# Attention and two MLP layers on one core: layer two's second products in seven partial products of 256 columns

## The chip, the cores and the metric

One core of a Trainium2 chip runs the whole program in one launch. The time is device time in microseconds (us); the kernel before took 741.88 us, the median of 3 runs (741.71 to 742.18).

## The reference

```python
def reference(**kw):                       # cut to the shapes and the arithmetic
    # attention: 2 batches x 8 heads x 768 positions x 64; a query sees the keys of its own cluster
    attn_out = _attn_ref(q, k, v, centroids)
    x = attn_out.transpose(0, 2, 1, 3).reshape(1536, 512)
    h = x @ moe_w_in                       # 1536x512 @ 512x2048, layer one
    x = np.maximum(0.01 * h, h) @ moe_w_out        # @ 2048x512
    h = x @ moe2_w_in                      # layer two, the same shapes
    r = np.maximum(h, 0.0)
    return (r * r) @ moe2_w_out
```

All of it is float32. The kernel splits each operand of a product into a high part (fp32r) and a low part and adds three products, high x high, high x low and low x high.

## The kernel before, in words

After the attention come two layers, `m` = 0 and 1. The 2048 hidden columns are 16 blocks `f` of 128, taken in pairs (`f`, `f` + 1); the 1536 rows are three parts `b` of 512. For each pair and each `b` the first product gives a hidden tile of 128 x 512 in one of four PSUM banks U, V, W, X (tag `h0` to `h3`); the activation splits it into `gh` and `gl`; the second product goes from these into four banks `o0` to `o3`, and a flush adds them to the sums `acc` in SBUF.

Three forms of a pair exist. A plain pair computes everything directly. A quad pair (`quad`, layer two from `f` = 2 on) computes the first product of `b` = 0 and 1 with seven products in place of eight (the Strassen-Winograd form of a 2 x 2 block product: P1 to P7, with differences of the inputs `th`, `tl` and of the weights, block `(m, f, 2)`), and its second products directly: `g2` issues for each hidden tile four slices of three matmuls, 512 columns wide. A pair of `seven` (layer one, `f` = 4 to 14) does the same for the second products too: differences T1 to T4 of the hidden tiles B11, B12, B21, B22, seven products M1 to M7 with a fourth weight block `(m, f, 3)`, and after each product the bank's contents, a partial sum, are added to `acc` (r1 to r7, two each). `b` = 2 is always direct: u0, u1 are its hidden tiles, o0 to o3 its second products, f0 to f3 their flushes. In the plain and quad forms the second products of `b` = 2 are done in the next pair (`behind`).

In `seven` the order of all engines is written out in one string of names: SEVEN_FIRST, then SEVEN_REST. Every engine takes its own instructions in that order. A name ending in `h` writes `gh` on ScalarE, in `f` the full value on ScalarE, in `l` the low part `gl` (GpSimd for B11, T1, T2, T3, VectorE otherwise); k and a are copies and sums of partial products on ScalarE and VectorE; T1 to T4 and the r and f flushes are on VectorE. n0.0 to n3.4 prepare the weight blocks of the next pair (c: this pair, l: the one after): for blocks 0 and 1 the steps are .0 the load, .1 "mag" on ScalarE and "low" on GpSimd (of the raw words in `wraw`), .2 the join of both on VectorE, .3 the high part on ScalarE, .4 the low part on GpSimd; for blocks 2 and 3 (differences) .0 is four sums on GpSimd, .1 the high part, .2 the low part. The two layers' activations read:

```python
        def prelu(out, x):                                   # in seven, before
            nc.scalar.activation(out=out, in_=x, func=AF.Prelu, alpha=0.01)
        def square():                                        # in acts, layer two
            nc.vector.scalar_tensor_tensor(
                out=h, in0=h, scalar=0.0, in1=t, op0=ALU.max, op1=ALU.mult)
```

In layer two the activation of `acts` is a relu on ScalarE into a buffer `t`, the square on VectorE, the high part on ScalarE, the low part on VectorE. In layer one the stationary operand of the second product is the weight slice and the moving one is the hidden tile (out: columns x rows); in layer two it is a slice of 128 rows of `gh` or `gl`, and the moving one is the weight (out: rows x columns), so that the result can be stored as it is.

Of the kernel before, what the change touches and what calls it, by code (L numbers as in the profile page):

```python
# [80 lines left out]
) + SEVEN_REST + " h4.0 h4.1"  # L81
DOTS = {(0, 0): 0, (0, 1): 1, (1, 0): 2}
# [3 lines left out]
def attention_moe_moe_kernel(  # L86
# [26 lines left out]
    SEVEN = (4, 6, 8, 10, 12, 14)  # L113
# [44 lines left out]
    for m in range(2):  # L158
        for f in range(0, NF, 2):
            blocks += [(m, f, 0), (m, f, 1)]  # L160
            if f >= PLAIN[m] * 2:
                blocks.append((m, f, 2))
            if m == 0 and f in SEVEN:
                blocks.append((m, f, 3))
# [842 lines left out]
    def last_rows(b):  # L1007

        banks = [(ps_o, "o0"), (ps_o, "o1"), (ps_o, "o2"), (ps_l, "o3")]
        pair = [(parts.pop((1, b, f)), weights[1, NF - 2, f % 2]) for f in (NF - 2, NF - 1)]  # L1010
        for o in range(4):
            ts = slice(o * 128, (o + 1) * 128)
            for i in range(2 if o == 3 else 1):
                c = slice(i * N // 2, (i + 1) * N // 2) if o == 3 else slice(0, N)
                if i:
                    ps = bank(0)
                else:
                    pool, tag = banks[o]
                    ps = pool.tile([128, N], F32, tag=tag, name="o")
                ps = ps[:, 0 : c.stop - c.start]  # L1020
                n = 0
                for (gh, gl), (wh, wl) in pair:
                    w = slice(DM + c.start, DM + c.stop)
                    for l, r in (
                        (gh[:, ts], wh[:, w]), (gh[:, ts], wl[:, w]), (gl[:, ts], wh[:, w])
                    ):
                        nc.tensor.matmul(out=ps, lhsT=l, rhs=r, start=(n == 0), stop=(n == 5))  # L1027
                        n += 1
                flush(1, b, NF // 2 - 1, o, ps, c)

# [30 lines left out]
    def quad(m, f):  # L1061
        f0, f1, s = ((m, f, j) for j in range(3))
        k2 = range(2)

        def p(out, w, x, first):
            product(out, [w(k) for k in k2], [x(k) for k in k2], first)

        def add(out, a, b):
            nc.vector.tensor_tensor(out=out, in0=a, in1=b, op=ALU.add)

        U, V, W, X = (bank(i) for i in range(4))

        def first():
            p(U, lambda k: w_in(f0, k), lambda k: x_in(k, 0), True)
            p1 = tmp()
            nc.scalar.copy(out=p1, in_=U)
            p(V, lambda k: w_in(f0, 2 + k), lambda k: x_in(2 + k, 0), True)
            add(V, V, p1)
            act(m, 0, f, V)

        kept = []

        def second():
            for q, i, o, fresh in ((U, 2, 1, False), (W, 0, 0, True)):
                p(q, lambda k: w_in(s, i + k), lambda k: t_in(o, k), fresh)
                kept.append(tmp())
                nc.scalar.copy(out=kept[-1], in_=q)

        def third():
            u2, p5 = kept  # L1090
            p(U, lambda k: w_in(s, 4 + k), lambda k: t_in(2, k), False)
            add(X, U, p5)
            x = acts(m, 1, f + 1, X)
            w = acts(m, 1, f, W)
            u = acts(m, 0, f + 1, U)
            if m:
                x.pop(0)()
            p(W, lambda k: w_in(s, 6 + k), lambda k: x_in(2 + k, 1), False)
            if m:
                x.pop(0)()  # L1100
            x.pop(0)()
            add(W, W, u2)
            if m:
                w.pop(0)()
            p(U, lambda k: w_in(f1, 2 + k), lambda k: t_in(3, k), False)
            if m:
                u.pop(0)()
            x.pop(0)()
            for q in (w, u):
                if m:  # L1110
                    q.pop(0)()
                q.pop(0)()
            w.pop(0)()
            u.pop(0)()

        return first, second, third

    def seven(f, prev, after, later):

        f0, f1, si, so = ((0, f, j) for j in range(4))  # L1120
# [45 lines left out]
        def prelu(out, x):  # L1166
            nc.scalar.activation(out=out, in_=x, func=AF.Prelu, alpha=0.01)
# [3 lines left out]
        def high(n, x, active=False):  # L1171
            hi[n] = gg.tile([128, N], F32R, tag="gh", name="gh")
            lo[n] = gg.tile([128, N], F32R, tag="gl", name="gl")
            if active:
                prelu(hi[n], x)
            else:
                nc.scalar.copy(out=hi[n], in_=x)
# [4 lines left out]
        def active(n, x, sbuf=False):  # L1182
            full[n] = tmp("t", 3) if sbuf else x
            prelu(full[n], x)
# [32 lines left out]
        def second(out, ws, g, fresh, stop=True):  # L1217
            wh, wl = ws
            mm = ((wh, hi[g]), (wh, lo[g]), (wl, hi[g]))
            for i, (l, r) in enumerate(mm):  # L1220
                nc.tensor.matmul(  # L1221
                    out=out, lhsT=l, rhs=r, start=(fresh and i == 0), stop=(stop and i == 2),
                    skip_group_check=True,
                )

        def w_out(block, c):
            return tuple(w[:, c : c + 128] for w in weights[block])

        def seventh(q, block, c, g, fresh):
            if fresh:  # L1230
                for j in range(2):
                    i = 2 * "AB".index(q) + j
                    st[q, j] = (ps_l if i == 3 else ps_o).tile(
                        [128, N], F32, tag=f"o{i}", name="o"
                    )
            for j in range(2):
                second(st[q, j], w_out(block, c + 128 * j), g, fresh)

        for name, q, block, c, g, b, half in (
# [8 lines left out]
            for j in range(2):  # L1248
                g = f // 2 if f < NF - 2 or name in "2347" else 1
                ops[f"r{name}.{j}"] = lambda q=q, j=j, b=b, g=g, o=2 * half + j: flush(  # L1250
                    0, b, g, o, st[q, j], later=x_low if b == 0 and o > 1 else None
                )

        def last(o):
            ps = st["o", o] = bank((3, 2, 3, 2)[o])
            c = DM + o * 128
            second(ps, w_out(f0, c), "u0", True, False)
            second(ps, w_out(f1, c), "u1", False)

# [85 lines left out]
    def step_list(m, f, prev):  # L1345
# [9 lines left out]
        if f < 2 * PLAIN[m]:  # L1355
            seq = [unit(0, 0), unit(0, 1)]
            if behind:
                seq[1:1] = behind[:1]
                seq += behind[1:]
            seq += [unit(1, 0), out_of(0, 0)]  # L1360
            if m:
                held = []

                def start():
                    held.extend(acts(m, 1, f + 1, g1(m, 1, f + 1)))
                    for g in held[:2]:
                        g()

                def out_and_end():
                    out_of(0, 1)()  # L1370
                    for g in held[2:]:
                        g()

                seq += [start, out_and_end]
            else:
                seq += [unit(1, 1), out_of(0, 1)]
            seq += [unit(2, 0), out_of(1, 0), unit(2, 1), out_of(1, 1)]
            return seq, tail

        first, second, third = quad(m, f)  # L1380
        seq = [
            first, behind[0], second, behind[1], third,
            out_of(0, 0), unit(2, 0), out_of(0, 1), unit(2, 1), out_of(1, 0), out_of(1, 1),
        ]
        if f == NF - 2:
            return seq + [lambda: last_rows(2)], []
# [44 lines left out]
    for m in range(2):  # L1431
        turn = 0
        for f in range(0, NF, 2):
# [13 lines left out]
            if m == 0 and f in SEVEN:  # L1447
                seven(f, prev, after, later)
# [3 lines left out]
            for i, step in enumerate(seq):  # L1452
# [12 lines left out]
                if m == 0 and i == 8 and f + 2 == SEVEN[0]:  # L1465
# [50 lines left out]
```

## Time and profile before

| | |
|---|---|
| median of 3 runs | 741.88 us (741.71 to 742.18) |
| the profiled execution | 742.35 us, of which 740.4 us span |
| TensorE busy | 733.9 us (99%) |
| VectorE, ScalarE, GpSimd busy | 545.7, 454.8, 503.7 us |
| granted TensorE clock | 1.00 of full speed over the span |

The profile follows one execution. An engine is busy while one of its instructions is under way; matmuls overlap in the pipe, so their rate is read from one start to the next, not from their duration. The chain of waits goes back from the last instruction to what released each step. In the lists by time, what stands in brackets at a row's end is the idle time before it and what ended it. Layer one ends 485.46 us after the span's start; layer two's pairs begin at 485.46 (plain), 512.66, 543.94, 575.22, 606.50, 637.78, 669.06 and 700.34.

### The profile page before, as it was taken

The numbers are of one execution on the slowest core, as the hardware profiler recorded it, in microseconds if no ns is written. First come the engines' busy times: TensorE is split into PE (matmuls) and PEld (weight loads), VectorE is DVE, ScalarE is ACT, GpSimd is POOL, SyncE is SP. The second block draws the span as 40 slices with busy tenths as digits, with TensorE's granted clock in tenths as the row PEclk, the third lists the DMA queues.
The fourth block names the chain that finished last, engine by engine and source line by source line (L and its number), as shares of the span: only waits on it lengthen the run. The fifth ranks groups of instructions, "written<-read, shape, count | busy, mean of one in ns | idle before, by whom it ended". The sixth has DMA issues, their size and how long they took to land.

```text
span 740.4 us, 11210 instructions
## 1 busy us (share of the span) xinstructions
PE 733.9 (99%) x4012; PEld 640.5 (87%) x4012; DVE 545.7 (74%) x856; ACT 454.8 (61%) x841; POOL 503.7 (68%) x471
## 2 busy tenths in 40 slices
PE   9999999999999999999999999999999999999998
PEld 8999999999998888888888888888888888888886
DVE  7999999999997535477776866887666666676655
ACT  7988988988998564446365363657634435443330
POOL 6999999999957648776787877899534343343400
PEclk9999999999999999999999999999999999999999
DMA  5694474572603311112121131111312112121004
GB/s 149 166 215 120 108 187 110 110 186 67 172 1 116 113 58 58 57 58 82 62 86 57 58 114 57 58 58 57 112 45 73 58 58 85 44 99 58 1 0 171
DMA packets 16727, 65.52 MB, mean 88 GB/s; under 512 B 3120, under 2 KB 4272, under 8 KB 11680
## 3 DMA queue, kind: packets, MB, share of 16 engines
q1 hardware_dynamic: 16672, 64.81, 29.7%
q8 instruction: 32, 0.52, 0.3%
q14 instruction: 23, 0.19, 0.1%
HBM read 43.02 MB, written 3.15 MB: 62 GB/s over the span
## 4 chain that ended last, share of the span: by engine, by line
PE 94%; POOL 2%; DVE 2%; ACT 1%; issue 1%; DMA 0%; POOLq 0%; ACTq 0%
PE h L919 33%; PE o L997 21%; PE A L583 8%; PE S L486 8%; PE o L1221 8%; PE T L548 7%; PE h L1221 4%; PE S L356 2%; PE warm L296 1%; PE o L1027 1%; ACT e L518 1%; POOL e L535 1%; DVE el L565 1%; DVE nm L508 0%; DMA hb<-spl 0%
## 5 line engine op out<-in xcount | busy, mean ns | idle before, releaser
L173 POOL TENSOR_TENSOR wl<-wt,wh 128x1024 fp32r<-128x1024 f32 x31 | 75.9, 2448 | 59.8 <-ACT wh L172 59.1
L1037 DVE TENSOR_TENSOR acc<-o,acc 128x512 f32<-128x512 f32 x160 | 103.6, 684 | 11.9 <-PE o L997 11.9
L919 PE MATMUL h<-xh,wl 128*128 128x512 f32 x288 | 112.4, 390 | 0.0
L919 PE MATMUL h<-xl,wh 128*128 128x512 f32 x288 | 112.3, 390 | 0.0
L919 PE MATMUL h<-xh,wh 128*128 128x512 f32 x288 | 112.1, 391 | 0.0
L565 DVE TENSOR_TENSOR el<-T,eh 128x512 fp32r<-128x512 f32 x144 | 94.5, 682 | 2.8 <-ACT eh L559 2.1
L535 POOL TENSOR_SCALAR e<-e,r 128x768 f32<-128x768 f32 x96 | 86.2, 908 | 12.7 <-PE T L548 6.8
L508 DVE TENSOR_REDUCE nm<-S 128x1 f32<-128x768 f32 x96 | 90.8, 947 | 3.7 <-PE S L356 1.9
L518 ACT ACTIVATE e<-S,nm 128x768 f32<-128x768 f32 x96 | 87.2, 908 | 10.0 <-DVE ds L384 3.6
L486 PE MATMUL S<-hb 128*128 128x384 f32 (+1 forms) x384 | 89.5, 347 | 0.5 <-DMA hb<-spl 0.4
L559 ACT CAST eh<-T 128x512 fp32r<-128x512 f32 x144 | 79.5, 590 | 8.9 <-PE T L548 8.7
L583 PE MATMUL A<-eh,vv 128*128 128x256 f32 x288 | 80.4, 308 | 0.6 <-DVE xt L605 0.6
L548 PE MATMUL T<-ident,e 128*128 128x128 f32 x576 | 79.7, 274 | 0.6 <-POOL e L535 0.6
L583 PE MATMUL A<-el,vv 128*128 128x256 f32 x288 | 73.0, 283 | 0.2 <-DVE el L565 0.2
L968 DVE TENSOR_TENSOR gl<-h,gh 128x512 fp32r<-128x512 f32 x60 | 40.8, 690 | 43.8 <-ACT h L963 24.5
L548 PEld LDWEIGHTS T<-ident,e 128*128 128x128 f32 x576 | 68.9, 143 | 3.6 <-POOL e L535 0.7
L997 PE MATMUL o<-wh,gl 128*128 128x512 f32 x184 | 71.7, 390 | 0.0
L997 PE MATMUL o<-wh,gh 128*128 128x512 f32 x184 | 71.7, 389 | 0.0
L997 PE MATMUL o<-wl,gh 128*128 128x512 f32 x184 | 71.7, 389 | 0.0
L173 POOL TENSOR_TENSOR wl<-ws,wh 128x1024 fp32r<-128x1024 f32 x18 | 43.3, 2403 | 41.3 <-ACT wh L172 41.3
L953 ACT ACTIVATE t<-h 128x512 f32<-128x512 f32 x48 | 28.1, 600 | 67.5 <-PE h L919 33.9
L919 PEld LDWEIGHTS h<-xh,wh 128*128 128x128 f32 x288 | 54.1, 188 | 11.9 <-DVE gl L1180 0.9
(187 smaller groups left out, 1763.7 us busy)
## 6 DMA issues: line engine op xcount, KB each, us to landing
wraw<-w SPq DMA_DIRECT2D x32, 1024.0 KB, 4.7
hb<-spl SPq DMA_DIRECT2D x14, 576.0 KB, 4.7
hb<-spl SPq DMA_DIRECT2D x42, 192.0 KB, 5.1
rqk<-qk SPq DMA_DIRECT2D x16, 384.0 KB, 3.9
rv<-v SPq DMA_DIRECT2D x8, 384.0 KB, 3.3
out<-q SPq DMA_DIRECT2D x11, 256.0 KB, 2.9
hb<-st SPq DMA_DIRECT2D x56, 24.0 KB, 2.1
hb<-hb SPq DMA_DIRECT2D x5, 144.0 KB, 8.3
```

What stands on the lines that cost most here:

```text
L173: return lambda eng=nc.gpsimd: eng.tensor_tensor(out=wl, in0=t, in1=wh.bitcast(F32), op=ALU.subtract)
L486: nc.tensor.matmul(out=s[:, c, 0:HALF], lhsT=hb[0:k, a, i * 128 : (i + 1) * 128], rhs=hb[0:k, b, c * HALF : (c + 1) * HALF], start=(a == 0 ...
L508: nc.vector.tensor_reduce(out=n, in_=s_t[t][:, :, 0:HALF], axis=AX.XY, op=ALU.max, negate=True)
L518: nc.scalar.activation(out=e.rearrange("p (a b) -> p a b", a=2), in_=s_t.pop(t)[:, :, 0:HALF], func=AF.Exp, bias=n_t.pop(t), scale=1.0, ac ...
L535: nc.gpsimd.tensor_scalar(out=e_t[t], in0=e_t[t], scalar1=r_t[t // 2][:, t % 2 : t % 2 + 1], scalar2=1.0, op0=ALU.mult, op1=ALU.mult,)
L548: nc.tensor.transpose(T[:, o : o + 128], e_t[2 * u + b][:, kc * 128 : (kc + 1) * 128], ident)
L565: nc.vector.tensor_tensor(out=el[:, 2 * g : 2 * g + 2, :].rearrange("p a b -> p (a b)"), in0=T_t.pop((u, g)), in1=eh[:, 2 * g : 2 * g + 2, ...
L583: nc.tensor.matmul(out=A, lhsT=w, rhs=m[:, kc, :], start=(kc == 0 and i == 0), stop=(kc == KC - 1 and i == 1),)
L919: nc.tensor.matmul(out=out, lhsT=l, rhs=r, start=(first and i == 0), stop=(i == n - 1), skip_group_check=not first,)
L997: nc.tensor.matmul(out=outs[o], lhsT=l, rhs=r, start=(first and i == 0), stop=(last and i == 2),)
L1037: nc.vector.tensor_tensor(out=a, in0=ps, in1=a, op=ALU.add)
L1221: nc.tensor.matmul(out=out, lhsT=l, rhs=r, start=(fresh and i == 0), stop=(stop and i == 2), skip_group_check=True,)
```

## The change

Layer two's seven pairs from `f` = 2 on go through `seven` in place of `quad`, which is removed, and so is `last_rows`, which did the end of the last pair. In `seven` for `m` = 1 the activation is a relu in place in PSUM and then squares on ScalarE: one into `gh`, one into the full value. The seven second products take 128 rows of `gh` as the stationary operand and 256 columns of the weight as the moving one, and write two row slices side by side into one bank; a flush then adds a bank of 2 x 256 columns to `acc`. The second pair's order (SEVEN_SEAM) holds the second products of the plain pair (bh0, bh1) and its own fourth weight block (c3); the last pair's (SEVEN_END) has no next weights and ends with the last row slice in two halves (e0, e1); the other five take SEVEN_TWO + SEVEN_REST.

```diff
+SEVEN_TWO = SEVEN_FIRST.replace("B11h B11f P5 k5", "B11h P5 k5 B11f")
+SEVEN_SEAM = (
+    "c3.0 P1 k1 P2 aV B11h bh0 P6 k6 B11f P5 k5 B11l c3.1 c3.2 bh1 P7 aX B22h B22f n0.1 P3 aW B12f P4 B21h "
+    "B21f n0.2 T1 T3 B21l T2 n1.0 T2h T1h T2l T1l n0.3 n0.4 T4 u0 u0h u0f u0l T3h T3l n1.1 n1.2 n1.3 n1.4 "
+) + SEVEN_REST
+SEVEN_END = " ".join(x for x in SEVEN_TWO.split() if x[0] != "n") + (
+    " M1 M2 r1.0 r1.1 r2.0 r2.1 B22l u1 u1h u1f u1l M6 M5 r6.0 r5.0 r5.1 r6.1 o0 f0 M3 r3.0 T4h T4l r3.1 "
+    "o1 f1 M7 r7.0 r7.1 o2 f2 M4 r4.0 r4.1 e0 e1"
+)
...
-    SEVEN = (4, 6, 8, 10, 12, 14)
+    SEVEN = tuple((0, f) for f in range(4, NF, 2)) + tuple((1, f) for f in range(2, NF, 2))
...
-    def seven(f, prev, after, later):
+    def seven(m, f, prev, after, later):
...
-        def prelu(out, x):
-            nc.scalar.activation(out=out, in_=x, func=AF.Prelu, alpha=0.01)
+        def active_to(out, x):
+            if m:
+                nc.scalar.activation(out=out, in_=x, func=AF.Square)
+            else:
+                nc.scalar.activation(out=out, in_=x, func=AF.Prelu, alpha=0.01)
+
+        def relu(x):
+            if m:
+                nc.scalar.activation(out=x, in_=x, func=AF.Relu)
...
             if active:
-                prelu(hi[n], x)
+                relu(x)
+                active_to(hi[n], x)
...
         def active(n, x, sbuf=False):
+            if n not in hi:
+                relu(x)
             full[n] = tmp("t", 3) if sbuf else x
-            prelu(full[n], x)
+            active_to(full[n], x)
...
-        def second(out, ws, g, fresh, stop=True):
+        def second(out, ws, g, fresh, stop=True, o=0):
             wh, wl = ws
             mm = ((wh, hi[g]), (wh, lo[g]), (wl, hi[g]))
+            if m:
+                gh, gl = (x[g][:, o * 128 : (o + 1) * 128] for x in (hi, lo))
+                mm = ((gh, wh), (gh, wl), (gl, wh))
...
             for j in range(2):
-                second(st[q, j], w_out(block, c + 128 * j), g, fresh)
+                if not m:
+                    second(st[q, j], w_out(block, c + 128 * j), g, fresh)
+                    continue
+                for i in range(2):
+                    second(
+                        st[q, j][:, i * K : (i + 1) * K], w_out(block, c, K), g,
+                        fresh and i == 0, o=2 * j + i,
+                    )
+
+        def flushed(b, j, half, ps, end):
+            c = slice(half * K, (half + 1) * K)
+            a = acc[:, b, 2 * j : 2 * j + 2, c]
+            ps = ps.rearrange("p (a b) -> p a b", a=2)
+            if not end:
+                add(a, ps, a)
+                return
...
-        order = SEVEN_PLAIN if f < 2 * PLAIN[0] else SEVEN_QUAD if f < NF - 2 else SEVEN_LAST
-        for name in order.split():
+        order = {
+            (0, 4): SEVEN_PLAIN, (0, NF - 2): SEVEN_LAST, (1, 2): SEVEN_SEAM, (1, NF - 2): SEVEN_END
+        }
+        for name in order.get((m, f), (SEVEN_QUAD, SEVEN_TWO + SEVEN_REST)[m]).split():
             ops[name]()
```

What the change does to the order on three engines follows. The names are the program's tiles, `o` for the second products' banks, `h` for U to X; lines below 1060 of the changed kernel are some 9 to 14 off those before.

TensorE, where the first products of a layer-two pair end and the second begin, before:

```order
L919 MATMUL h<-xh,wh 128x512
L919 MATMUL h<-xl,wh 128x512
L919 MATMUL h<-xh,wl 128x512
L997 MATMUL o<-wh,gh 128x512
L997 MATMUL o<-wl,gh 128x512
L997 MATMUL o<-wh,gl 128x512
```

The same place with the change (the end of u0, the start of M1):

```order
L928 MATMUL h<-xh,wh 128x512
L928 MATMUL h<-xl,wh 128x512
L928 MATMUL h<-xh,wl 128x512
L1162 MATMUL o<-wh,gh 128x256
L1162 MATMUL o<-wl,gh 128x256
L1162 MATMUL o<-wh,gl 128x256
```

The second products have become 256 columns wide, twelve to a product.

VectorE in the second pair of layer two, before (`h<-h,t` is the square, `gl` the low part, `wt<-wt,wraw` the join of the second weight block of the next pair, `acc` the flushes):

```order
L968 TENSOR_TENSOR gl<-h,gh 128x512
L956 SCALAR_TENSOR_TENSOR h<-h,t 128x512 x2
L968 TENSOR_TENSOR gl<-h,gh 128x512 x2
L211 SCALAR_TENSOR_TENSOR wt<-wt,wraw 128x1024
L956 SCALAR_TENSOR_TENSOR h<-h,t 128x512
L968 TENSOR_TENSOR gl<-h,gh 128x512
L1037 TENSOR_TENSOR acc<-o,acc 128x512 x4
```

The same pair with the change (`h<-h,q` are aV, aX and aW, the first join is n0.2, `t<-t`, `t<-h,t`, `t<-h,t` and `h<-h,t` are T1, T3, T2 and T4, `gl` is B21l and then u0l, the second join is n1.2, `acc` is r1.0 to r2.1):

```order
L1055 TENSOR_TENSOR h<-h,q 128x512 x3
L220 SCALAR_TENSOR_TENSOR wt<-wt,wraw 128x1024
L1055 TENSOR_TENSOR t<-t 128x512
L1055 TENSOR_TENSOR t<-h,t 128x512
L1116 TENSOR_TENSOR gl<-h,gh 128x512
L1055 TENSOR_TENSOR t<-h,t 128x512
L1055 TENSOR_TENSOR h<-h,t 128x512
L1116 TENSOR_TENSOR gl<-h,gh 128x512
L220 SCALAR_TENSOR_TENSOR wt<-wt,wraw 128x1024
L1055 TENSOR_TENSOR acc<-o,acc 128x2x256 x4
```

The squares are gone, four differences have come, and the second join stands right ahead of the flush of the first second product.

GpSimd in the second pair, before (`wl<-ws,wh` the low part of a difference block, `tl` of an input difference, `wraw` the step "low"):

```order
L173 TENSOR_TENSOR wl<-ws,wh 128x1024
L1303 TENSOR_TENSOR tl<-q,th 128x512
L205 TENSOR_SCALAR wraw<-wraw 128x1024
L173 TENSOR_TENSOR wl<-wt,wh 128x1024
L205 TENSOR_SCALAR wraw<-wraw 128x1024
L253 TENSOR_TENSOR ws<-wt 128x256
```

With the change (four sums c3.0, `gl<-t,gh` is B11l, then T2l and T1l, then T3l; the second `wraw` is the "low" of n1.1):

```order
L262 TENSOR_TENSOR ws<-wt 128x256
L262 TENSOR_TENSOR ws<-ws,wt 128x256
L262 TENSOR_TENSOR ws<-wt 128x256
L262 TENSOR_TENSOR ws<-wt,ws 128x256
L1116 TENSOR_TENSOR gl<-t,gh 128x512
L182 TENSOR_TENSOR wl<-ws,wh 128x1024
L214 TENSOR_SCALAR wraw<-wraw 128x1024
L1116 TENSOR_TENSOR gl<-t,gh 128x512 x2
L182 TENSOR_TENSOR wl<-wt,wh 128x1024
L1116 TENSOR_TENSOR gl<-t,gh 128x512
L214 TENSOR_SCALAR wraw<-wraw 128x1024
L182 TENSOR_TENSOR wl<-wt,wh 128x1024
```

Between the two "low" steps, where one subtraction stood, there now stand four, three of them of T1 to T3.

## Rows read from the trace of the kernel before

**Rows 1.** The page: busy time by engine, and the chain that ended last.
```profile
PE 733.9 (99%) x4012; PEld 640.5 (87%) x4012; DVE 545.7 (74%) x856; ACT 454.8 (61%) x841; POOL 503.7 (68%) x471
...
PE 94%; POOL 2%; DVE 2%; ACT 1%; issue 1%; DMA 0%; POOLq 0%; ACTq 0%
```
**Rows 2.** Stretches: us, busy PE, PEld, DVE, ACT, POOL, clock, DMA share, GB/s.
```profile
425.33:455.32 29.99, 29.99 (x133) 24.70 (x132) 21.31 (x32) 15.74 (x24) 24.07 (x19) 1.00 0.20 71
...
512.66:543.94 31.28, 31.28 (x139) 25.91 (x139) 20.51 (x27) 18.48 (x30) 19.31 (x14) 1.00 0.20 68
543.94:575.22 31.28, 31.28 (x139) 25.93 (x139) 20.43 (x30) 13.65 (x20) 12.31 (x10) 1.00 0.20 68
```
**Rows 3.** TensorE in order of time, the kernel's end: start us, duration us, instruction.
```profile
735.31 0.39 PE L1027 MATMUL o<-wh,gl 128*128 128x512 f32 x1
735.53 0.28 PE L1027 MATMUL o<-wh,gh 128*128 128x256 f32 x1
...
736.85 0.28 PE L1027 MATMUL h<-wh,gl 128*128 128x256 f32 x1
```
**Rows 4.** ScalarE in order of time, layer one's pair that begins at 425.33.
```profile
430.09 0.60 ACT L1167 ACTIVATE gh<-h 128x512 fp32r<-128x512 f32 x1
430.58 0.60 ACT L1167 ACTIVATE t<-h 128x512 f32<-128x512 f32 x1
...
433.12 0.60 ACT L1167 ACTIVATE gh<-h 128x512 fp32r<-128x512 f32 x1 [0.52 <-DVE h L1127]
...
434.42 0.60 ACT L1167 ACTIVATE t<-h 128x512 f32<-128x512 f32 x1 [0.22 <-DVE h L1127]
...
436.06 1.14 ACT L198 ACTIVATE wt<-wraw 128x1024 f32<-128x1024 f32 x1
437.09 1.35 ACT L1177 CAST gh<-t 128x512 fp32r<-128x512 f32 x2
```
**Rows 5.** VectorE in order of time, the same pair; the last row is layer two's second pair.
```profile
432.39 0.70 DVE L1127 TENSOR_TENSOR h<-h,q 128x512 f32<-128x512 f32 x1 [3.37 <-PE h L919]
...
435.12 0.69 DVE L1127 TENSOR_TENSOR t<-t 128x512 f32<-128x512 f32 x1 [0.73 <-POOL wl L173]
...
437.65 1.22 DVE L211 SCALAR_TENSOR_TENSOR wt<-wt,wraw 128x1024 int32<-128x1024 int32 x1
...
449.43 0.69 DVE L1180 TENSOR_TENSOR gl<-h,gh 128x512 fp32r<-128x512 f32 x1 [0.69 <-ACT gh L1177]
...
451.23 1.28 DVE L1037 TENSOR_TENSOR acc<-o,acc 128x512 f32<-128x512 f32 x2
...
531.59 1.23 DVE L211 SCALAR_TENSOR_TENSOR wt<-wt,wraw 128x1024 int32<-128x1024 int32 x1 [0.40 <-ACT wt L198]
```
**Rows 6.** GpSimd in order of time, the same two pairs.
```profile
431.26 1.30 POOL L1180 TENSOR_TENSOR gl<-t,gh 128x512 fp32r<-128x512 f32 x1 [0.36 <-ACT t L1167]
432.68 2.39 POOL L173 TENSOR_TENSOR wl<-wt,wh 128x1024 fp32r<-128x1024 f32 x1
435.16 1.65 POOL L205 TENSOR_SCALAR wraw<-wraw 128x1024 int32<-128x1024 uint32 x1
437.79 4.76 POOL L1180 TENSOR_TENSOR gl<-t,gh 128x512 fp32r<-128x512 f32 x3 [0.98 <-ACT gh L1177]
442.51 2.39 POOL L173 TENSOR_TENSOR wl<-wt,wh 128x1024 fp32r<-128x1024 f32 x1
...
519.75 1.11 POOL L205 TENSOR_SCALAR wraw<-wraw 128x1024 int32<-128x1024 uint32 x1
...
528.56 1.12 POOL L205 TENSOR_SCALAR wraw<-wraw 128x1024 int32<-128x1024 uint32 x1
...
532.89 0.74 POOL L253 TENSOR_TENSOR ws<-wt 128x256 f32<-128x256 f32 x1 [3.21 <-DVE wt L211]
```
**Rows 7.** The chain of waits, its last computing step: start us, us, what.
```profile
737.16 0.42 DVE q L1055
```
**Rows 8.** DMA issues: xcount, KB each, median us to landing.
```profile
wraw<-w SPq DMA_DIRECT2D x32, 1024.0 KB, 4.7
```

More of the change, by code (lines that the diff above doesn't have):

```diff
@@ L162, in attention_moe_moe_kernel @@
                 blocks.append((m, f, 2))
-            if m == 0 and f in SEVEN:
+            if (m, f) in SEVEN:
                 blocks.append((m, f, 3))
@@ L1005, in g2 @@
                 flush(m, b, f // 2, o, outs[o])
[L1007 to L1029, printed above, removed]
     def flush(m, b, g, o, ps, part=slice(0, 512), later=None):
@@ L1059, in attention_moe_moe_kernel @@
     x_low = {}
[L1061 to L1116, printed above, removed]
-    def seven(f, prev, after, later):
-        f0, f1, si, so = ((0, f, j) for j in range(4))
+    def seven(m, f, prev, after, later):
+        f0, f1, si, so = ((m, f, j) for j in range(4))
         k2, ks = range(2), range(HP)
@@ L1201, in unit @@
         def unit(j):
-            st[f"u{j}"] = bank(1)
+            st[f"u{j}"] = bank(1 + j * m)
             product(
@@ L1224, in second, with w_out @@
                 )
-        def w_out(block, c):
-            return tuple(w[:, c : c + 128] for w in weights[block])
+        def w_out(block, c, n=128):
+            return tuple(w[:, c : c + n] for w in weights[block])
         def seventh(q, block, c, g, fresh):
@@ L1236, in seventh @@
             for j in range(2):
-                second(st[q, j], w_out(block, c + 128 * j), g, fresh)
+                if not m:
[13 more added lines that the diff above has]
+                return
+            ob = tmp().rearrange("p (a b) -> p a b", a=2)
+            add(ob, ps, a)
+            r = b * N + j * 256
+            nc.sync.dma_start(
+                out=out[r : r + 256, c].rearrange("(a p) c -> p a c", p=128), in_=ob
+            )
         for name, q, block, c, g, b, half in (
@@ L1252, in seven, with end @@
                 )
+                if m:
+                    end = f == NF - 2 and name in "2347"
+                    ops[f"r{name}.{j}"] = lambda q=q, j=j, b=b, half=half, end=end: flushed(
+                        b, j, half, st[q, j], end
+                    )
         def last(o):
             ps = st["o", o] = bank((3, 2, 3, 2)[o])
-            c = DM + o * 128
-            second(ps, w_out(f0, c), "u0", True, False)
-            second(ps, w_out(f1, c), "u1", False)
+            c, n = (DM, DM) if m else (DM + o * 128, 128)
+            second(ps, w_out(f0, c, n), "u0", True, False, o)
+            second(ps, w_out(f1, c, n), "u1", False, True, o)
+        def end(i):
+            ps = bank((2, 1)[i])[:, 0:K]
+            c = slice(i * K, (i + 1) * K)
+            second(ps, w_out(f0, DM + i * K, K), "u0", True, False, 3)
+            second(ps, w_out(f1, DM + i * K, K), "u1", False, True, 3)
+            flush(m, 2, f // 2, 3, ps, c)
+        for i in range(2):
+            ops[f"e{i}"] = lambda i=i: end(i)
         for o in range(4):
             ops[f"o{o}"] = lambda o=o: last(o)
-            ops[f"f{o}"] = lambda o=o: flush(0, 2, f // 2, o, st["o", o], later=x_low)
+            ops[f"f{o}"] = lambda o=o: flush(m, 2, f // 2, o, st["o", o], later=x_low)
             ops[f"x0.{o}"] = lambda o=o: x_low[0, o](nc.vector)
@@ L1265, in seven @@
             ops[f"bh{i}"] = lambda q=q: g2(*q)
-        for c, base in (("n", after), ("l", later), ("c", (0, f))):
+        for c, base in (("n", after), ("l", later), ("c", (m, f))):
             for k in range(4):
@@ L1354, in step_list, with start, out_and_end @@
         tail = [(m, 2, f), (m, 2, f + 1)]
[L1355 to L1386, printed above, removed]
+        seq = [unit(0, 0), unit(0, 1)]
+        if behind:
+            seq[1:1] = behind[:1]
+            seq += behind[1:]
+        seq += [unit(1, 0), out_of(0, 0)]
+        if m:
+            held = []
+            def start():
+                held.extend(acts(m, 1, f + 1, g1(m, 1, f + 1)))
+                for g in held[:2]:
+                    g()
+            def out_and_end():
+                out_of(0, 1)()
+                for g in held[2:]:
+                    g()
+            seq += [start, out_and_end]
+        else:
+            seq += [unit(1, 1), out_of(0, 1)]
+        seq += [unit(2, 0), out_of(1, 0), unit(2, 1), out_of(1, 1)]
         return seq, tail
@@ L1446, in attention_moe_moe_kernel @@
             later = pair_after(*after)
-            if m == 0 and f in SEVEN:
-                seven(f, prev, after, later)
+            if (m, f) in SEVEN:
+                seven(m, f, prev, after, later)
                 prev = []
@@ L1464, in attention_moe_moe_kernel @@
                     piece((*later, k - 3) if k > 2 else (*after, k), j, *eng)
-                if m == 0 and i == 8 and f + 2 == SEVEN[0]:
+                if (m, f + 2) == SEVEN[0] and i == 8:
                     piece((*after, 3), 0)
```

## Prediction

> **What bounds the kernel now.** I read the page first. TensorE is busy for 733.9 us, 99% of the span, and holds 94% of the chain that ended last [rows 1]. The table by stretches says the same of the two layers. A pair of blocks in layer two takes 31.28 us with TensorE busy throughout at granted clock 1.00, and layer one's pairs of seven products take 29.99 us in the same way; VectorE, ScalarE and GpSimd are busy for about 21, 14 to 18 and 12 to 24 us of that [rows 2]. So time is TensorE's instructions times their spacing, as long as nobody makes it wait. The duration of one matmul (390 or 280 ns) is its length in the pipe; what it costs is the distance to the next start. That is 31.28 / 138 = 0.2267 us for 512 columns, and 0.120 us for 256 columns, from the last twelve matmuls of the kernel: eleven steps from 735.53 to 736.85 [rows 3]. Their operands are those the change uses: a stationary slice of gh, moving weights.
>
> **TensorE's work.** A pair of quad computes its second products with 48 matmuls of 512 columns (4 calls of g2, 4 output slices, 3 terms); the change computes them with 7 products of 12 matmuls of 256 columns. Everything else on TensorE stays in number. 48 x 0.2267 = 10.88, 84 x 0.120 = 10.08: 0.80 us a pair, 5.6 us over seven pairs. One eighth of the second product's multiplications is gone, but half-wide matmuls give 40% of that back (42 matmuls of 512 columns would have been 9.52 us).
>
> Here the Trainium skill would promise more. "TensorE: Matmul & The Clock Gate", Back-to-back issue gap, gives N / 2.4 + 2.5 ns warm: 215.8 ns for 512 columns and 109.2 ns for 256. By that the saving would be an estimated 8.3 us over 336 and 588 matmuls. The trace has both steps, 226.7 and 120 ns, and they decide.
>
> **What hangs on the other engines.** Layer two gets layer one's scheme: 14 flushes instead of 8 a pair, four differences T1 to T4, a fourth weight block split on GpSimd. Layer one carries all that without a gap [rows 2]. New is ScalarE: relu in place, then a square into gh, then a square into the full value, where layer one has two independent Prelus 0.49 us apart (430.09, 430.58). The first square waits for the relu: 0.60 + 0.03 + 0.49 + 0.49, that is 1.6 us instead of 1.0 [rows 4]. I price the relu at its 0.60 us and a square, which the trace does not have, like a Prelu of the same shape; between 0.5 and 0.7 us each the pair's ScalarE work stays under 24 us of 30, so only latency counts. I follow that in two places. Times t count from a pair's first matmul (P1).
>
> **The second pair (SEVEN_SEAM).** TensorE reaches M6 at t = 23.28, after 15 groups of six matmuls of 512 columns (1.36 us each; P4, the eleventh, ends at 14.96) and M1 and M2 (12 x 0.120 = 1.44 us each). M6 adds to the bank of M1, so it needs r1.0 done on VectorE. On VectorE the word-join of the next weight block (n1.2) stands directly ahead of r1.0, and that join needs the GpSimd step "low" of the same block, which GpSimd's list has behind T2l, T1l, a weight subtraction and T3l. How late is it?
> - ScalarE after P7 (ends 12.24): the sum aX on VectorE, 0.26 after P7 as in layer one and 0.70 long, to 13.2 [rows 5]; B22 in three steps from there; the weight magnitude n0.1 at 14.85, 1.03 us to the next start [rows 4]; B12's two steps from 15.9; B21's three steps from 17.0, ending at 18.7. P4 had ended 3.7 us before; this is backlog.
> - VectorE: B21l at 18.7, T2 0.6 later, done at 20.0 [rows 5]. ScalarE: T2h to 20.6.
> - GpSimd, which has nothing it may do earlier: T2l, T1l, the weight subtraction, T3l and low at 1.30, 1.30, 2.40, 1.30 and 1.10 us, each starting 0.04 before the end of the one ahead [rows 6]: from 20.7 to 28.0.
> - VectorE: join 1.22, then r1.0 0.68 [rows 5]: done at 29.8.
>
> M6 is 6.5 us late. If ScalarE had no backlog at all (relu of B21 at 15.16), B21 would end at 16.9 and the same chain gives 28.0, 4.8 us late: my lower bound. The upper is 7.0, a square of 0.7 us. What GpSimd does earlier in that pair does not decide: its old work, the first low included, ends at t = 8.2 (520.86); four new sums of 0.74 us, B11l and c3.2 (1.30 and 2.40 us) make it free by t = 15 [rows 6]. Before the change the same low began at 528.56 (t = 15.9) and the join at 531.59 (t = 18.9), and no product of that time waited for a flush behind it [rows 5, 6].
>
> **The five pairs that follow SEVEN_TWO + SEVEN_REST.** By T1h ScalarE has four more relus of 0.63 us, less some 0.9 us that it idled there in layer one, 0.52 and 0.22 of it in front of B22h and B12f: T1h starts at t = 13.2 instead of 11.76 [rows 4]. Two points of TensorE are near:
> - M6 (17.84) needs r1.0, behind T1, T2, join, T4 and u0l. If T1 starts as soon as B12f is done (10.7), r1.0 ends at 17.3, in time. But low is free to start at 10.7 too, when the subtraction ahead of it ends. In layer one T1 had to wait for a GpSimd subtraction and started 0.04 us after it, and the low behind it took 1.65 instead of 1.10 us [rows 5, 6]: these two do not run together. If low comes first, T1 is 1 us late, the later join then stands behind T1l (layer one has the reverse case, T1l behind a join: three such subtractions took 4.76 us where one alone takes 1.30 [rows 6]), and r1.0 ends at 18.2: 0.4 us late.
> - M4 (27.68) needs r7.0, which stands behind T4l; T4h stands on ScalarE behind the split of the next sums, which waits for GpSimd's four sums after T3l and a subtraction. In layer one T4l started at t = 24.1 (449.43) and r7.0 at 25.9 (451.23) [rows 5]; with 1.3 to 1.6 us more r7.0 ends at 27.9 to 28.2: 0.2 to 0.5 us late, less what M6 has already lost.
>
> The sum a pair is 0 to 1.0 us; I take 0.4, 2.0 us in five pairs.
>
> The Trainium skill, "SBUF — State Buffer", SBUF: two separate sides, has a rule for the first point: the port pair shared by VectorE and GpSimd is locked for a whole instruction when a VectorE operation reads two SBUF inputs. The trace agrees: T1 and the join have two SBUF inputs, and just these collide.
>
> **The rest.** Layer one's pairs take 29.99 us where 132 x 0.2267 is 29.92; the same contact over seven pairs is 0.4 us. The last pair has no weight work, so T4h and r1.0 come early; its tail ends as before with six matmuls of 256 columns, a 0.42 us flush and a store [rows 7]. More output stores in the last 8 us and two more flushes cost 0 to 0.5; I take 0.1. The weight loads keep their number and land 4.7 us after issue, well before their use [rows 8]. No table load joins ScalarE's list.
>
> **Sum.** -5.6 + 6.5 + 2.0 + 0.4 + 0.1 = +3.4 us. The profiled execution took 742.35 us, 740.4 of span and 1.9 around it, giving 745.7; the median of the runs shown is 741.88, and I state the time against that: 745.3.
>
> **Rivals.**
> - The saving arrives: **736.7** (-5.6 + 0.4). For it: TensorE is the bound everywhere, and layer one's pairs hide the same work. It needs M6 of the second pair on time, which means 6.5 us less in a chain that is all in rows; only if a part of it is not in that order on the chip. Chance 0.11.
> - Only the second pair stalls, T1 always goes ahead of low and M4 finds r7.0 done: -5.6 + 6.5 + 0.5 = +1.4, or +0.5 with 5.6 us at the seam: about **743.0**. For it: the margin at T1 is 0.02 us either way, and the ScalarE steps of 0.49 us may overlap a little more. Chance 0.25.
> - Every one of the five pairs loses at T1 and at M4, 1.0 us each, low always ahead of T1: -5.6 + 6.5 + 5.0 + 0.5 = +6.4, **748.3**. For it: squares slower than Prelu. Chance 0.12.
> - The forecast, second pair and a part of the rest: 743.5 to 747.5, chance 0.52.
>
> The low end of all bounds is -5.6 + 4.8 = -0.8 us, 741.1; the high end 7.0 + 5.0 + 1.0 - 5.6 = +7.4, 749.3. The range 742.2 to 748.0 leaves out the first rival, a part of the second and of the third. What a measurement tells from no change is 0.2%, 1.5 us. Faster by more: the first rival, 0.11. Within: most of the second rival, 0.19. Slower: 0.70.
>
> **What would show it.** In the profile after: 256-column matmuls with steps of 0.120 us; in the second pair of layer two one gap of 5 to 7 us in front of a group of 256-column matmuls, ended by VectorE's acc, and VectorE idle before the join until GpSimd's low; in the next five pairs gaps under 1 us at the third and the last product; a pair of about 30.9 us there. No gap in the second pair, or one under 4 us, makes the forecast wrong; pairs of 30.5 us make the second rival right.

## The result and the profile after

The changed kernel takes **747.31 us** (median of 6 runs, 746.58 to 747.71) where the kernel before took 741.81 us beside it: a ratio of 1.0072, 95% interval 1.0059 to 1.0085, 5.5 us slower. The forecast was 745.3 us, 742.2 to 748.0, slower with a chance of 0.70. The direction and the place of the loss were right; the size was 2 us short.

The profiled execution spans 745.4 us, 5.0 more than before. Its page (busy time, then busy tenths and granted clock in 40 slices):

```profile
PE 732.4 (98%) x4264; PEld 648.9 (87%) x4264; DVE 554.5 (74%) x877; ACT 492.0 (66%) x911; POOL 582.2 (78%) x534
...
PE   9999999999999999999999999999789999999998
...
PEclk9999999999999999999999999999989999999999
...
PE 84%; ACT 5%; DVE 5%; POOL 4%; issue 2%; POOLq 0%; DVEq 0%; ACTq 0%
```

Against [rows 1], TensorE's share of the chain falls from 94 to 84%, and VectorE, ScalarE and GpSimd together hold 14% of it where they held 5. Two neighbouring slices hold a hole, and the clock's row dips in the second of them. The stretches (length; busy PE, PEld, DVE, ACT, POOL; clock, DMA share, GB/s) answer to [rows 2]: the 31.44 us of the second pair that end with the start of f = 4, the pair of f = 4, two later ones, the last.

```profile
525.60:557.04 31.44, 25.09 (x142) 22.32 (x141) 20.03 (x30) 15.89 (x24) 20.45 (x18) 0.89 0.20 68
557.04:588.43 31.39, 31.02 (x175) 26.71 (x175) 22.79 (x32) 19.04 (x30) 23.01 (x18) 1.00 0.20 68
619.18:649.94 30.76, 30.76 (x175) 26.88 (x175) 21.29 (x32) 18.84 (x30) 23.78 (x19) 1.00 0.19 69
649.94:680.72 30.78, 30.78 (x175) 26.88 (x175) 21.29 (x32) 18.82 (x30) 23.77 (x19) 1.00 0.19 69
711.48:742.12 30.64, 30.63 (x180) 27.06 (x179) 19.73 (x31) 13.95 (x25) 7.57 (x5) 1.00 0.23 84
```

Pairs of 31.28 us became 30.76: the saving is there, less some 0.3 us. The second pair holds the loss. TensorE in order of time at M6 (start, duration; in brackets the idle time before and what ended it):

```profile
535.70 0.39 PE L928 MATMUL h<-xh,wl 128*128 128x512 f32 x1
542.43 0.55 PE L1162 MATMUL o<-wh,gh 128*128 128x256 f32 x1 [6.35 <-DVE acc L1055]
542.78 0.42 PE L1162 MATMUL o<-wl,gh 128*128 128x256 f32 x1
...
545.99 0.37 PE L1162 MATMUL o<-wl,gh 128*128 128x256 f32 x1
546.20 0.28 PE L1162 MATMUL o<-wh,gl 128*128 128x256 f32 x1
546.32 0.28 PE L1162 MATMUL o<-wh,gh 128*128 128x256 f32 x1
```

From 535.70 to 542.43 are 6.73 us where 0.227 were due: 6.5 us lost in front of M6. Behind it come a step of 0.35 us, steps of 0.21 to 0.22 us up to 546.20, and steps of 0.12 us after. Stretches of the same place show why (the last figures are clock, DMA share, GB/s):

```profile
536.00:539.40 3.40, 0.09 (x1) 0.00 (x0) 0.69 (x1) 1.71 (x3) 3.31 (x3) 0.99 0.00 0
539.40:542.40 3.00, 0.00 (x0) 0.00 (x0) 1.94 (x3) 0.68 (x1) 1.03 (x1) 0.50 0.00 0
542.40:546.20 3.80, 3.77 (x18) 3.80 (x18) 3.47 (x6) 1.94 (x4) 3.27 (x3) 0.50 0.82 276
546.20:550.00 3.80, 3.80 (x27) 3.54 (x27) 3.34 (x6) 1.53 (x2) 2.64 (x4) 1.00 0.00 0
```

While TensorE stood still, the granted clock fell from 1.00 (2.4 GHz) to 0.50 (1.2 GHz), and it rose again only at 546.20. From 542.43 to 546.20 are seventeen steps of 256 columns (the stretch counts the matmul that starts at its end too): 3.77 us in place of 17 x 0.120 = 2.04, so 1.7 us more. "TensorE: Matmul & The Clock Gate" of the Trainium skill, section Back-to-back issue gap, gives a step of N / 1.2 ns at the low clock, an estimated 213 ns for 256 columns; the rows agree.

The chain that the prediction wrote out is in the rows: GpSimd, then VectorE.

```profile
533.16 2.55 POOL L1116 TENSOR_TENSOR gl<-t,gh 128x512 fp32r<-128x512 f32 x2 [5.86 <-ACT gh L1113]
535.67 2.37 POOL L182 TENSOR_TENSOR wl<-wt,wh 128x1024 fp32r<-128x1024 f32 x1
538.00 1.26 POOL L1116 TENSOR_TENSOR gl<-t,gh 128x512 fp32r<-128x512 f32 x1
539.34 1.09 POOL L214 TENSOR_SCALAR wraw<-wraw 128x1024 int32<-128x1024 uint32 x1
```

```profile
540.46 1.23 DVE L220 SCALAR_TENSOR_TENSOR wt<-wt,wraw 128x1024 int32<-128x1024 int32 x1 [3.58 <-POOL wraw L214]
541.61 2.48 DVE L1055 TENSOR_TENSOR acc<-o,acc 128x512 f32<-128x512 f32 x4
```

These are T2l and T1l, a weight subtraction, T3l and low, then the join, for which VectorE idled 3.58 us, then r1.0. GpSimd had idled 5.86 us before T2h reached it.

**The balance.** -5.6 (TensorE's work), +6.5 (the wait), +1.7 (low clock), +2.2 (the other six pairs over 30.48 us, which is 90 x 0.2267 + 84 x 0.120: 0.9 for f = 4, four times 0.28, 0.16 for the last), together +4.8. Some 0.3 us more lie in the second pair: the third matmul of M2 starts at 531.88, 0.05 us behind the end of B21l, and two steps there take 0.23 us in place of 0.12; the rest is in its groups of six (last section). That makes 5.1 us, and between the spans there are 5.0. The tail changes by nothing: 3.26 us from the last flush to the end, 3.24 before.

### The profile page after: what moved, and what is told of

Its sections match the earlier page's. It is cut to its first block, busy times and chain, and to the rows that moved or that the text cites. A ratio compares the mean times of both kernels' runs of the same rounds, so it can differ in the third digit from the quotient of the medians.

```text
span 745.4 us, 11900 instructions
## 1 busy us (share of the span) xinstructions
PE 732.4 (98%) x4264; PEld 648.9 (87%) x4264; DVE 554.5 (74%) x877; ACT 492.0 (66%) x911; POOL 582.2 (78%) x534
## 4 chain that ended last, share of the span: by engine, by line
PE 84%; ACT 5%; DVE 5%; POOL 4%; issue 2%; POOLq 0%; DVEq 0%; ACTq 0%
PE h L928 28%; PE o L1162 16%; PE h L1162 9%; PE A L592 8%; PE S L495 7%; PE T L557 7%; PE o L1006 4%; PE S L365 1%; ACT e L527 1%; POOL tl L1281 1%; POOL wl L182 1%; DVE nm L517 1%; DVE xl L1030 1%; POOL ws L262 1%; PE warm L305 1%
## 5 line engine op out<-in xcount | busy, mean ns | idle before, releaser
L1116 POOL TENSOR_TENSOR gl<-t,gh 128x512 fp32r<-128x512 f32 x52 | 74.9, 1456 | 39.5 <-ACT gh L1113 28.6
L182 POOL TENSOR_TENSOR wl<-ws,wh 128x1024 fp32r<-128x1024 f32 x25 | 60.1, 2404 | 47.6 <-ACT wh L181 47.6
L1055 DVE TENSOR_TENSOR h<-h,q 128x512 f32<-128x512 f32 x36 | 25.2, 699 | 60.8 <-PE h L928 51.7
L1116 DVE TENSOR_TENSOR gl<-h,gh 128x512 fp32r<-128x512 f32 x65 | 44.5, 687 | 30.8 <-ACT h L1098 13.5
L207 ACT ACTIVATE wt<-wraw 128x1024 f32<-128x1024 f32 (+1 forms) x33 | 36.7, 1111 | 46.1 <-POOL ws L262 42.7
L928 PEld LDWEIGHTS h<-xh,wl 128*128 128x128 f32 x288 | 54.1, 188 | 11.3
L495 PEld LDWEIGHTS S<-hb 128*128 128x128 f32 (+1 forms) x384 | 62.3, 189 | 1.7 <-ACT e L527 1.1
```

What stands on the lines that cost most here:

```text
L182: return lambda eng=nc.gpsimd: eng.tensor_tensor(out=wl, in0=t, in1=wh.bitcast(F32), op=ALU.subtract)
L495: nc.tensor.matmul(out=s[:, c, 0:HALF], lhsT=hb[0:k, a, i * 128 : (i + 1) * 128], rhs=hb[0:k, b, c * HALF : (c + 1) * HALF], start=(a == 0 ...
L928: nc.tensor.matmul(out=out, lhsT=l, rhs=r, start=(first and i == 0), stop=(i == n - 1), skip_group_check=not first,)
L1116: eng.tensor_tensor(out=lo[n], in0=full[n], in1=hi[n].bitcast(F32), op=ALU.subtract)
```

## The experiments

All are edits of the changed kernel. The ratios are to the kernel before, timed beside them on the same chip.

**E1: is the low clock a cost of its own?** TensorE gets work for the time in which it stood.

```diff
-            product(st[f"u{j}"], ...)
+            for _ in range(3 if (m, f, j) == (1, 2, 1) else 1):
+                product(st[f"u{j}"], ...)
```

> Compared with the changed kernel (747.3 us). In the second pair of layer two TensorE's twelve matmuls of u1 (2.72 us) are issued three times over, so that TensorE works on for 5.4 us of the 6.5 us for which it stood in front of M6; the result of u1 is the same. Theory: the wait has two costs, the 6.5 us themselves and 1.6 us behind them, because the granted clock fell to half during the wait and eighteen matmuls of 256 columns ran at 0.21 us instead of 0.12. With TensorE at work the first cost stays (the wait shrinks to 0.9 to 1.1 us, M6 starts at the same time), the clock stays at 1.00 and the 1.6 us go: 745.7 us (745.4 to 746.0), less than the changed kernel though it does 24 matmuls more. Rival: the low clock is no cost of its own, since VectorE's flushes after M6 set the pace there anyway: 747.3 us. Second rival: u1 is on the path, and three of them push it back: 748 us or more.

Measured: 745.40 us (744.67 to 745.90), ratio 1.0047 (1.0033 to 1.0060), 1.9 us under the changed kernel with 24 matmuls more. TensorE around M6, and the stretches there:

```profile
540.19 0.39 PE L928 MATMUL h<-xh,wl 128*128 128x512 f32 x1
541.56 0.36 PE L1163 MATMUL o<-wh,gh 128*128 128x256 f32 x1 [0.98 <-DVE acc L1055]
541.75 0.28 PE L1163 MATMUL o<-wl,gh 128*128 128x256 f32 x1
541.87 0.28 PE L1163 MATMUL o<-wh,gl 128*128 128x256 f32 x1
```

```profile
539.00:541.00 2.00, 1.58 (x7) 0.96 (x6) 1.42 (x2) 0.16 (x1) 0.55 (x1) 1.00 0.00 0
541.00:543.00 2.00, 1.44 (x12) 1.48 (x13) 2.00 (x4) 1.91 (x4) 1.03 (x1) 1.00 0.61 131
```

M6 comes no earlier against the rest of the pair (30.1 us after the pair's first matmul, 30.0 in the changed kernel), but the clock stays at 1.00 and the steps behind it are 0.12 us at once. The wait and the low clock are two costs, and this run separates them. (The expectation counts eighteen slow matmuls and 1.6 us; the rows have seventeen and 1.7.)

**E2: is the join in front of r1.0 the cause?** Only its place changes, with the steps that hang on it.

```diff
-    "... T3h T3l n1.1 n1.2 n1.3 n1.4 "
-) + SEVEN_REST
+    "... T3h T3l "
+) + SEVEN_REST.replace("r2.1", "r2.1 n1.1 n1.2 n1.3 n1.4")
```

> In the second pair's order the four steps of the next weight block (magnitude and low, join, cast, subtraction) move from in front of M1 to behind the flushes r1.0 to r2.1. GpSimd's order stays as it was. Theory of the prediction, taken at its word: the join in front of r1.0 holds M6; with it gone M6 waits at most for r1.0 behind u0l, some 1.7 us, the rest of the 6.5 us and the 1.6 us of low clock go, and the kernel takes about 741 us. Rival: the join is only the last link. GpSimd and ScalarE are behind by as much, and the steps that now come behind the join (B22l, u1h, u1f, the flushes r6 and r5) are late in its place: the wait falls into three or four pieces of 0.8 to 2 us with a sum of 6 to 7 us, and only the low clock's cost goes: 745.5 to 747.5 us.

Measured: 747.23 us (745.54 to 747.29), ratio 1.0064 (1.0052 to 1.0077): no gain. M6 is 4.8 us earlier, and the time is lost behind it. TensorE's waits:

```profile
538.07 0.35 PE L1162 MATMUL o<-wh,gh 128*128 128x256 f32 x1 [1.54 <-DVE acc L1055]
...
542.99 0.47 PE L1162 MATMUL h<-wh,gh 128*128 128x512 f32 x1 [1.82 <-DVE gl L1116]
...
544.55 0.80 PE L1162 MATMUL h<-wh,gh 128*128 128x512 f32 x1 [0.27 <-ACT gh L1096]
...
546.96 0.58 PE L1162 MATMUL o<-wh,gh 128*128 128x256 f32 x1 [0.40 <-DVE acc L1055]
```

The rival holds in its main point: the join is the last link only, and its late low delays B22l and u1 in place of r1.0. In its sums it does not. The four waits add up to 4.0 us, not 6 to 7, and the low clock, which both readings had gone, took what that gave back: the granted clock was 0.50 from 544 to 550, and the pair takes 44.1 us where it took 44.5. I had expected the clock to stay up through several short waits. In one of the five executions its mean was 0.998 where the others have 0.995, and that one took 745.54 us, 1.3 to 1.8 us less than the others.

```profile
543.00:544.00 1.00, 1.00 (x3) 0.52 (x3) 0.00 (x0) 0.91 (x3) 0.60 (x1) 0.68 0.92 131
544.00:547.00 3.00, 2.33 (x5) 0.83 (x4) 1.98 (x4) 0.99 (x2) 2.92 (x3) 0.50 0.72 306
547.00:550.20 3.20, 3.20 (x14) 3.10 (x15) 2.33 (x4) 1.51 (x2) 2.05 (x4) 0.50 0.00 0
```

**E3: the five pairs.** Three moves in their order.

```diff
+LAYER_TWO = SEVEN_TWO.replace("n1.2 T4 u0 T2l u0h u0f u0l", "T4 u0 T2l u0h u0f n1.2") + SEVEN_REST.replace(
+    "M2 r1.0", "M2 r1.0 u0l"
+).replace("n2.1 n2.2 o0 f0 M3 r3.0 T4h", "T4h n2.1 n2.2 o0 f0 M3 r3.0")
```

> Only the order of the five pairs after the second changes: VectorE's join goes behind T4 and the high parts of u0, u0l behind r1.0, and T4h on ScalarE goes in front of the cast of the next sums; the second and the last pair stay. Theory: the waits in front of M6 (0.53 and 0.18 us in the pair of f=4) and in front of M4 (0.18 us in each of the others, with 0.07 at the group before) come from these three places, so they go, and the kernel is 1.0 to 1.5 us faster than the changed one: 746.0 us (745.7 to 746.4). Rival: VectorE's and GpSimd's two-input operations collide elsewhere in the new order, the waits move to M5 or M7, and the time stays at 747.3 us or rises by up to 2 us.

Measured: 746.02 us (745.34 to 746.26), ratio 1.0051 (1.0038 to 1.0064), 1.6 us less by the ratios, whose intervals overlap; the trace is clearer: f = 4 takes 30.72 us in place of 31.39 and the pairs after it 30.58 in place of 30.76. The only wait left in layer two is the second pair's:

```profile
PE o L1165 <- DVE acc L1058: 6.3, 1, 6.3
```

**E4 and E5: the second pair in another order, and both orders.** Each step of a weight block stands behind the split or flush that the next product needs:

```diff
-SEVEN_SEAM = (...)
+SEVEN_SEAM = (
+    "c3.0 P1 k1 P2 aV B11h bh0 P6 k6 B11f P5 k5 B11l bh1 P7 c3.1 n0.1 aX B22h B22f P3 aW B12f P4 B21h n0.2 "
+    "c3.2 B21f T1 T3 n1.0 T2 B21l T1h T4 T1l T2h u0 u0h T2l u0f B22l u0l T3h n0.3 M1 M2 r1.0 r2.0 r2.1 u1 "
+    "n1.1 u1h r1.1 u1f u1l n1.2 M6 T3l T4h M5 r5.0 r5.1 n0.4 r6.0 r6.1 o0 f0 T4l M3 r3.0 n1.3 r3.1 o1 f1 "
+    "n2.0 M7 r7.0 r7.1 o2 f2 n2.1 M4 n1.4 r4.0 l0.0 n2.2 r4.1 o3 f3 n3.0"
+)
```

> Compared with the changed kernel (747.3 us). Only the order of the second pair changes: every step of a weight block (magnitude, low, join, cast, subtraction, sums) stands behind the step that the next product waits for, from the head of the pair to its end; SEVEN_TWO, SEVEN_REST and SEVEN_END stay. Theory: the second pair's loss is the order in which three engines do their work, not the amount of it, so the 6.5 us in front of M6 and the 1.6 us of low clock both go and nothing comes in their place above 0.5 us: 739.2 us (738.7 to 740.5), faster than the kernel before. Rival: the work itself is too much for the engines in that pair; the waits go to other products and to the pair that follows, as they did when the join alone was moved, and the time stays between 744 and 747.5 us.

> The second pair's new order and the new order of the five pairs after it, together. Theory: the two gains are of different pairs and add: 8.1 and 1.3 us off 747.3 us, 737.9 us (737.2 to 739.0); what is left over the 5.6 us of TensorE's saving is the slip of a few tenths a pair. Rival: the new second pair hands the five pairs a later start of their weight steps, and one of the two gains is lost: 739 to 741 us.

Measured: E4 738.63 us (738.47 to 739.23), ratio 0.9956 (0.9942 to 0.9969), just under the expected range. E5 **737.62 us** (737.07 to 738.14), ratio 0.9942 (0.9930 to 0.9955): by the ratios 4.3 us faster than the kernel before and 1.0072 - 0.9942 = 1.3%, 9.6 us, faster than the changed one. Stretches of E5: the 30.86 us of the second pair that end with the start of f = 4, the pair of f = 4, a later one.

```profile
518.00:548.86 30.86, 30.86 (x175) 26.88 (x174) 21.62 (x32) 20.50 (x33) 25.56 (x22) 1.00 0.20 69
548.86:579.47 30.61, 30.61 (x176) 26.90 (x175) 22.31 (x32) 19.58 (x31) 25.95 (x22) 1.00 0.20 69
610.05:640.63 30.58, 30.58 (x176) 26.96 (x175) 22.40 (x32) 18.87 (x31) 24.13 (x19) 1.00 0.19 70
```

TensorE is busy throughout, and every engine has as many instructions as in the changed kernel. The whole second pair takes 36.4 us where the changed kernel's takes 44.5. So the loss was the order, not the amount of work.

**E6: how much is the order's tail alone?** The head up to T1l stays as in the changed kernel; the weight steps from n0.3 on stand late.

```diff
-    "... T2l T1l n0.3 n0.4 T4 u0 u0h u0f u0l T3h T3l n1.1 n1.2 n1.3 n1.4 "
-) + SEVEN_REST
+    "... T2l T1l T4 u0 u0h u0f u0l T3h n0.3 M1 M2 r1.0 r1.1 r2.0 r2.1 B22l u1 n1.1 u1h u1f u1l n1.2 M6 T3l T4h "
+    "M5 n0.4 r6.0 r5.0 ... M3 r3.0 n1.3 r3.1 o1 f1 n2.0 M7 ... n2.1 M4 n1.4 r4.0 l0.0 n2.2 r4.1 o3 f3 n3.0"
+)
```

> The changed kernel's second pair with its head as it was, up to T1l; only the steps of weight blocks behind it (n0.3 to n3.0) move to later places, each behind the split that the next product waits for. Theory: the head carries a part of the loss of its own (T1 and the splits of B21 behind a magnitude and a join), so a wait of about 0.8 us stays in front of M6 and one of about 1.9 us later in the pair, no low clock: 741.5 us (740.8 to 742.8). Rival: the head costs nothing that the tail cannot hide: 739.2 us as with the whole order.

Measured: 741.67 us (741.27 to 742.08), ratio 0.9994 (0.9985 to 1.0003). Two waits are left, in front of M6 and later, with the clock at 1.00 in the pair:

```profile
536.74 0.36 PE L1164 MATMUL o<-wh,gh 128*128 128x256 f32 x1 [0.59 <-ACT wh L183]
...
543.10 0.39 PE L1164 MATMUL o<-wh,gh 128*128 128x256 f32 x1 [1.85 <-DVE acc L1057]
```

By the ratios the tail is worth 5.8 us, the low clock's share included, and what E4 does beyond it another 2.8. That is the head together with a few moves behind it (B22l ahead of M1, r1.1 behind u1h, n0.4 behind r5.1); what the head is worth alone was not tested.

**E7: ScalarE's relus.** They are left out in the pairs of seven, so hidden values below zero are squared too.

```diff
         def relu(x):
-            if m:
-                nc.scalar.activation(out=x, in_=x, func=AF.Relu)
+            pass
```

> The changed kernel without the relu in front of each square in the pairs of seven products of layer two (28 steps of 0.6 us on ScalarE and more at u0, u1; the output changes with it). Theory: the second pair's wait comes from the order on GpSimd and VectorE, to which relu adds under 1 us: 5.6 us of 6.5 stay, and the low clock with them; the small waits of the five pairs, which come from ScalarE's extra steps, go: 745.2 us (744.6 to 745.8). Rival: ScalarE's extra work is the root of the second pair's backlog: the wait falls under 3 us, the clock stays up, and the kernel takes 741 to 742 us.

Measured: 745.30 us (744.30 to 745.65), ratio 1.0043 (1.0030 to 1.0057). TensorE's one wait:

```profile
PE o L1161 <- DVE acc L1055: 5.7, 1, 5.7
```

Without relu the wait before M6 shortens by 0.6 us, and the five pairs have none. The relus set the small waits of the five pairs and a tenth of the large one.

**E8 and E9: which of E3's moves does it?** Both start from E4's kernel, whose five pairs take 30.77 us; E8 has only the move of T4h, E9 only the other two.

```diff
+LAYER_TWO = SEVEN_TWO + SEVEN_REST.replace("n2.1 n2.2 o0 f0 M3 r3.0 T4h", "T4h n2.1 n2.2 o0 f0 M3 r3.0")  # E8
+LAYER_TWO = SEVEN_TWO.replace("n1.2 T4 u0 T2l u0h u0f u0l", "T4 u0 T2l u0h u0f n1.2") + SEVEN_REST.replace("M2 r1.0", "M2 r1.0 u0l")  # E9
```

> The kernel with the second pair's new order (738.6 us), and of the three edits to the five pairs only one: T4h on ScalarE goes in front of the cast of the next sums. Theory: the 0.18 us that each of the five pairs still waits in front of M4 come from T4h standing behind that cast, which waits for GpSimd's four sums; they go, the pairs fall from 30.77 to 30.60 us, and M6 stays on time as it is there: 737.6 to 738.0 us. Rival, the forecast's reading: T1 and the join bring r1.0 late, so a wait in front of M6 of some 0.3 us takes the place, and the pairs stay above 30.75 us.

> The kernel with the second pair's new order, and of the three edits to the five pairs only the other two: VectorE's join behind T4, and u0l behind r1.0; T4h stays behind the cast. Theory: M6 is on time there without them, so they give nothing at M6, and since they put the join and with it the next cast later, the wait in front of M4 stays or grows to 0.2 to 0.5 us: pairs of 30.77 to 31.1 us, 738.6 to 740.2 us. Rival: T1 and join are what makes T4l late, and without their collision the wait in front of M4 goes: pairs of 30.6 us, 737.7 us.

Measured in one run each: E8 738.41 us, E9 740.54 us, each some 0.4 us above its expected range. The times of single runs move by half a us (the five of E4 reach from 738.47 to 739.23), so the traces decide. The same pair of E8, then of E9:

```profile
610.59:641.17 30.58, 30.58 (x176) 26.96 (x175) 21.57 (x32) 18.87 (x30) 23.79 (x19) 1.00 0.21 70
```

```profile
611.24:642.33 31.09, 30.82 (x176) 26.88 (x175) 22.13 (x32) 18.84 (x30) 24.09 (x19) 1.00 0.19 69
```

Moving T4h removes the wait in front of M4; moving the join and u0l alone lengthens it to 0.43 us. In the changed kernel T4h starts only behind the cast that waits for GpSimd's sums:

```profile
642.68 1.05 ACT L181 CAST wh<-ws 128x1024 fp32r<-128x1024 f32 x1 [3.85 <-POOL ws L262]
643.64 0.58 ACT L1113 CAST gh<-h 128x512 fp32r<-128x512 f32 x1
```

## Why the prediction was right in direction and 2 us short

- **TensorE's work, -5.6: right.** Steps of 0.120 us for 256 columns; E5 gets 4.3 us of it by its ratio, 4.7 by the spans.
- **The second pair, +6.5: right, and for the stated reason as far as the chain goes.** Measured 6.5 us. Counted from the pair's first matmul, at 512.42, T2l was forecast at t = 20.7 and came at 20.7, low's end at 28.0 (28.0), r1.0's end at 29.8 (29.9). What the chain did not say is that its last link alone is no lever: E2 moved the join, and the kernel was no faster. E4 and E6 moved the whole list of such steps. Two numbers of the working do not follow from their terms, and neither moves the forecast: 28.0 is 4.7 us behind 23.28, not 4.8, and 11.76 with four relus of 0.63 us less 0.9 is 13.4, not 13.2, where T1h did come (632.20 in the pair that begins at 619.02).
- **The low clock: the step that failed.** The sum priced the wait by its length alone. The 1.7 us behind it, shown in the rows and taken out by E1, are in no term, and they are most of the 2 us by which 745.3 fell short: the spans differ by 5.0 us where the sum has 3.4. The rest is that the profiled execution of before lay 0.5 us above its median, and that of the changed kernel did not.
- **The five pairs, +2.0, and the slip, +0.4: the sum right, the places half right.** Measured 2.2 us with the last pair. I had two points, M6 behind T1 and join, and M4 behind T4h. M6 was late only in the pair of f = 4, by 0.53 us: there low started ahead of T1, T1 took 1.34 us and the join behind T1l 2.34.

```profile
567.65 1.10 POOL L214 TENSOR_SCALAR wraw<-wraw 128x1024 int32<-128x1024 uint32 x1
...
567.94 1.34 DVE L1055 TENSOR_TENSOR t<-t 128x512 f32<-128x512 f32 x1 [2.00 <-ACT t L1096]
...
571.12 2.34 DVE L220 SCALAR_TENSOR_TENSOR wt<-wt,wraw 128x1024 int32<-128x1024 int32 x1
```

In the pairs after it T1 went first and low paid (1.61 us at 629.80), so M6 was on time. E4 has no wait at M6 in f = 4 either, with that pair's own order unchanged: it was handed over by the second pair. M4 was 0.18 us late in each of the others, for the reason given; E7 and E8 show both halves of it, relu and T4h's place.
- **The rivals.** "The saving arrives" (736.7) was what another order could reach: 737.6. "Only the second pair stalls" (743.0) missed the clock as well; "every pair loses 1.0 us" (748.3) came near the time for a wrong reason, since 1.7 us of clock stood in for pairs that lost 0.28.

## What to carry to other kernels

Price a long wait of TensorE twice: its length, and the matmuls behind it that run at the lower clock until it rises (here 6.5 + 1.7 us); spare matmuls in the wait bought the second part back. Where the last link of a chain is a step that nobody needs soon, look at the whole list of such steps on each engine: moving one made the kernel no faster, moving all behind the next product's needs gave 8.6 us. And take the length of a pair apart by trace before naming a culprit: of E3's three moves one brought the gain, and the other two without it did harm.

## What was not expected of the hardware

- The clock also fell under several short waits: in E2 TensorE idled 1.54 us, worked for 3.1 us, idled 1.82, and with the next two pauses (0.27 and 0.40 us) between matmuls it ran at 0.50 from 544 to 550. In E6, with waits of 0.59 and 1.85 us and 4.5 us of work between them, the mean granted clock of the run stayed at 1.00.
- Groups of six matmuls of 512 columns that stand between groups of 256 columns take 1.39 us, 0.232 a step, against 0.227 in [rows 3] and in the first products (12.24 us for 54). That is some 0.1 us a pair, about what E5's pairs of 30.58 us have over 30.48. The reason was not tested.
